# Value matmuls of a sparse attention step: four rows of two heads instead of two rows of four, with the rest of the step's jobs moved to other positions

## The chip, the cores and the metric

The kernel runs on one core of a Trainium2 chip. The metric is device time in microseconds (us). A core has the engines TensorE (PE; PEld is its weight load), VectorE (DVE), ScalarE (ACT), GpSimd (POOL) and SyncE (SP, which only issues DMAs here). Each works through its own instructions in order, and they wait for one another on semaphores.

## The reference

```python
scores = scale * np.matmul(q, k.transpose(0, 1, 3, 2))      # 4 batches, 8 heads, 768 tokens, 64 wide
mask = np.abs(blk_i - blk_j) <= 1                            # 24 blocks of 32 tokens
mask = mask | (blk_i == 0) | (blk_j == 0) | (blk_i == n_blocks - 1) | (blk_j == n_blocks - 1)
for qb in range(n_blocks):
    for kb in sampled_blocks[qb]:                            # three drawn blocks for each block of queries
        mask[qb * block:(qb + 1) * block, kb * block:(kb + 1) * block] = True
attn = softmax(np.where(mask, scores, -1e9))
x = (attn @ v) as (4 * 768, 8 * 64) tokens
xn = x / sqrt(mean(x * x) + 1e-06) * rms_g
out = (silu(xn @ w_gate) * (xn @ w_val)) @ w_out             # 512 -> 1536 -> 512
```

The drawn blocks differ by block of queries but not by batch or head.

## The kernel before

**Two stages.** Batch 0 is done densely with a mask (to about 78 us). Batches 1 to 3 are done sparsely, in 18 chunks of four query blocks (128 tokens): per batch five chunks of blocks 2 to 21, and one "wide" chunk of the blocks 0, 23, 1 and 22, of which 0 and 23 see all keys. The feed-forward network (FFN) of tokens that are ready runs between the attention work on PE, in both stages.

**FFN pieces.** `ffn_pieces` cuts the FFN of a group of chunks into pieces. `gate` (L737) is four matmuls of 128x128 weights with as many columns as the group has tokens (256, 384 or 512), then a tanh on ACT (L741); `val` (L748) is four more, and two DVE operations (L752 `u`, L756 `hps`); a quarter of `down` (L766) is three matmuls of 512 columns, its last one followed by an ACT copy (L771) and a store. A group of n chunks has 24 + 4n pieces. The chunks are grouped 2, 3, 4, 4, 3, 2. `enter` puts a group's pieces in a list, spread over the positions to the next group's entry; `position()`, called once at the end of each position, takes out as many as are due.

**The sparse loop** has a step for each chunk i and one more, 19 in all, and each step has ten positions. `do(n, f)` hangs a job f on position n; at each position the jobs run in the order in which they were hung, then `position()`. There is no scheduler: this order is the order on every engine. In step i stand, before the change:

- the values of chunk i−1 (L644): position 0 heads 0 to 3, position 1 heads 4 to 7. `values` takes one PSUM bank `op` for each call. For a narrow chunk each call is 32 matmuls with 128x32 weights (the exponentials of one query block) against 66 columns of gathered V, with the four query blocks in the four 32-column parts of the array; for a wide chunk it is 64.
- `normalise` (DVE, L669 and L670: the reciprocal and a product out of `op`) at positions 1 and 2; `squares` (ACT, L677) at 4, `rms_power` (POOL, L681 and L682) at 5, `x_scaled` (DVE, L698, and a transposing DMA on SP to the group's `xg`) at 7. The four chunks in `by_pe` (the last ones of two groups, and both of the last group) are turned by PE instead (`x_turned`, L707), at position 0 of the step after, the last chunk at position 9 of the last step.
- the scores of chunk i (L620), at positions 1 to 4 in four runs of two heads, or 1 to 8 in eight runs of one head (wide). A run is eight matmuls of 64 columns with whole 128x128 weights, and an exponential on ACT (L628).
- gathering for chunk i+1: K by DVE (`gather_k`, L475 on) and by ACT and POOL copies at register addresses (`sampled_k`, L485), Q by four DVE copies (`gather_q`, L500), V by indirect DMAs of POOL (`gather_v`, L512), whose first two blocks are for chunk i+2, at positions 6 and 7, into one of three buffers `vgs`.
- for the next batch: loads, casts of V on ACT, and turns of K and Q (six transposes on PE, L455, and an ACT copy) at positions 6 and 9.

A group enters at position 4 of the second step after its last chunk. PSUM has eight banks, which `bank` hands out in turn to `op`, `st`, `gp`, `vp`, `yp` and transposes.

```python
for h in range(4 * g, 4 * g + 4):
    ...
    if not wide:
        for w in range(2):
            for j in range(QB):
                mm(h, j, ex[:, j, w, :], vg[:, j, w, h, :], w, 2)
```

Of the kernel before, what the change touches and what calls it, by code (L numbers as in the profile page):

```python
# [9 lines left out]
FP32 = mybir.dt.float32  # L10
# [8 lines left out]
def kernel(  # L19
# [83 lines left out]
    def bank(shape, dtype, name):  # L103
        space, tag = ring[turn_of[0] % len(ring)]
        turn_of[0] += 1
        return space.tile(shape, dtype, name=name, tag=tag)
# [27 lines left out]
    def load_v(b, pr):  # L134
        t = vraw[(b, pr)] = ld.tile([P, 2, NC, D], FP32, name="vraw", tag="vraw", bufs=4)
        if b:
            nc.vector.memset(t[0:1, 0, 0, 0:1], 0.0)
        (nc.sync if b else nc.gpsimd).dma_start(
            out=t, in_=v[b, 2 * pr:2 * pr + 2].rearrange("e (p c) d -> p e c d", p=P))
# [491 lines left out]

    ops, stages, ssqs, rstds = {}, {}, {}, {}

    def values(i, g):
        b, qbs = chunks[i]
        wide = qbs[0] == 0
        op = bank([P, 512], FP32, "op")
        ops.setdefault(i, []).append(op)
        vg = vgs[i % 3].rearrange("p j (w h x) -> p j w h x", w=2, h=H)
        per = H // bursts(i)  # L640

        def mm(h, j, lhsT, rhs, n, of):
            at = (h % 4) * VW
            nc.tensor.matmul(out=op[j * BLK:(j + 1) * BLK, at:at + VW], lhsT=lhsT, rhs=rhs,  # L644
                             start=(n == 0), stop=(n == of - 1))

        for h in range(4 * g, 4 * g + 4):
            part = h // per
            ex = exs[(i, part // 4)][:, part % 4 * 512:(part % 4 + 1) * 512].rearrange(
                "p (h u w s) -> p h u w s", h=per, w=2, s=BLK)[:, h % per]  # L650
# [4 lines that stand above are left out]
                continue  # L655
            for n in range(NC):
                cc, w = divmod(n, 2)
                for j in range(2):
                    mm(h, j, ex[:, 2 * cc + j, w, :], Vs[b % 2][:, 2 * cc + w, h, :], n, NC)
                if n < 2:  # L660
                    for j in range(2, QB):
                        mm(h, j, ex[:, 4 + j, n, :], vg[:, j, n, h, :], n, 2)

    def normalise(i, g):
        if g == 0:
            stages[i] = work.tile([P, 2, DM], BF16, name="stage", tag="stage", bufs=2)[:, 0]
        rz = work.tile([P, 4], FP32, name="rz", tag="rz", bufs=2)
        res = ops[i][g][:, 0:4 * VW].rearrange("p (h x) -> p h x", x=VW)
        nc.vector.reciprocal(out=rz, in_=res[:, :, D])  # L669
        nc.vector.tensor_tensor(  # L670
            out=stages[i].rearrange("p (g h d) -> p g h d", g=2, h=4)[:, g],
            in0=res[:, :, 0:D], in1=rz.unsqueeze(2).to_broadcast([P, 4, D]), op=ALU.mult)

    def squares(i):
        ssqs[i] = work.tile([P, 1], FP32, name="ssq", tag="ssq", bufs=3)
        junk = work.tile([P, DM], BF16, name="junk", tag="junk", bufs=1)
        nc.scalar.activation(out=junk, in_=stages[i], func=AF.Square, accum_out=ssqs[i])  # L677

    def rms_power(i):
        rstds[i] = work.tile([P, 1], FP32, name="rstd", tag="rstd", bufs=3)  # L680
        nc.gpsimd.tensor_tensor(out=ssqs[i], in0=ssqs[i], in1=eps, op=ALU.add)  # L681
        nc.gpsimd.tensor_tensor(out=rstds[i], in0=ssqs[i], in1=mhalf[:, 0:1], op=ALU.pow)  # L682
# [5 lines left out]
    def x_scaled(i):  # L688
        g = group_of[i]
        at = (i - sgroups[g][0]) * P  # L690
        if at == 0:
            xgs[g] = work.tile([P, KD, TG], BF16, name="xg", tag="xg", bufs=2)
        xs = xss[i] = work.tile([P, DM], BF16, name="xs", tag="xs", bufs=3)
        if i in by_pe:
            nc.vector.tensor_scalar(out=xs, in0=stages[i], scalar1=rstds[i], scalar2=None,
                                    op0=ALU.mult)
            return
        nc.vector.scalar_tensor_tensor(  # L698
            out=xs, in0=stages[i], scalar=rstds[i], in1=gain, op0=ALU.mult, op1=ALU.mult)
        nc.sync.dma_start_transpose(out=xgs[g][:, :, at:at + P], in_=xs)  # L700
# [361 lines left out]
    NPOS = 10  # L1062
    entry = {}
    for g, m in enumerate(sgroups[:-1]):
        entry[(min(m[-1] + 2, NCH), 4)] = g

    def distance(i, n):

# [9 lines left out]
    for i in range(NCH + 1):  # L1078
        jobs = {}

        def do(n, f):
            jobs.setdefault(n, []).append(f)

        b, s = divmod(i, PB)
        b += 1
        nx = i + 1 if i + 1 < NCH else None
        if i == 0:
            do(0, late_pv)
            do(3, lambda: dense_scale(cur, 0))
            do(3, lambda: dense_scale(cur, 1))  # L1090
            do(5, lambda: dense_turn(cur, 0))
            do(6, lambda: dense_turn(cur, 1))
            do(6, lambda: enter_dense(cur, distance(0, 6)))
            do(4, lambda: nc.vector.memset(Qd[1], 0.0))
            do(3, lambda: load_kq(2, 3))
            do(7, lambda: gather_v(1, (2, 3)))
        else:
            do(0, lambda: values(i - 1, 0))
            do(1, lambda: normalise(i - 1, 0))
            do(1, lambda: values(i - 1, 1))  # L1100
            do(2, lambda: normalise(i - 1, 1))
            do(4, lambda: squares(i - 1))
            do(5, lambda: rms_power(i - 1))
            do(7, lambda: x_scaled(i - 1))
            if i == NCH:
                do(9, lambda: x_turned(i - 1))
            if i - 2 in by_pe:
                do(0, lambda: x_turned(i - 2))
        if i < NCH:
            n = bursts(i)  # L1110
            for part in range(n):
                do(1 + part, lambda part=part: scores(i, part))
        if b + 1 < B and s <= NP:
            if s < NP:
                do(9 if s == 0 else 0, lambda: cast_v(b + 1, s, act))
            if s > 0:
                do(6, lambda: turn(b + 1, s - 1, 0, act, True))
                do(9, lambda: turn(b + 1, s - 1, 1, act, True))
            if s == 0 and b == 1:
                do(8, lambda: nc.vector.memset(Vs[0][:, :, :, D:VW], 1.0))  # L1120
            if s == NP:
                do(0, lambda: table(b + 1))
        if nx is not None:
            at = 6 if nx == 1 else 0
            gk, gq = list(gather_k(nx, dve)), list(gather_q(nx, dve))
            if at == 0:
                for m, x in enumerate(gq):
                    do(3 + m * 2 // len(gq) * 2, x)
                do(4, gk[0])
                for x in gk[1:]:  # L1130
                    do(6, x)
            else:
                do(at, gk[0])
                for m, x in enumerate(gk[1:]):
                    do(at + 1 + m, x)
                for m, x in enumerate(gq):
                    do(at + 1 + m // 2, x)
            kact, kpool = sampled_k(nx, "act"), sampled_k(nx, "pool")
            for x in kpool:
                do(at, x)  # L1140
            for m, x in enumerate(kact):
                do(at + (m + 1) * (NPOS - 1 - at) // len(kact), x)
            if nx > 1:
                do(1, lambda: gather_v(nx, (2,)))
                do(2, lambda: gather_v(nx, (3,)))
            if nx + 1 < NCH:
                at = 6 if (nx + 1) % PB else 8
                do(at, lambda: gather_v(nx + 1, (0,)))
                do(at + 1, lambda: gather_v(nx + 1, (1,)))
        for m in range(min(6, len(by_need)) if i < 2 else 0):  # L1150
            do(m, next_address)

        bl, sl = divmod(i + 2, PB)
        if 0 < bl and bl + 2 < B and sl < NP:
            do(9, lambda: load_kq(bl + 2, sl))
        bv, sv = divmod(i + 3, PB)
        if 0 < bv and bv + 2 < B and sv < NP:
            do(7, lambda: load_v(bv + 2, sv))
        for n in range(NPOS):
            if (i, n) in entry:  # L1160
                g = entry[(i, n)]
                enter(ffn_pieces(xgs[g], sizes[g], chunk_store(sgroups[g])), distance(i, n))
            for x in jobs.get(n, ()):
                x()
            position()
# [35 lines left out]
```

## Time and profile before

| | |
|---|---|
| runs | 309.20, 309.18, 309.12 us; median 309.18 |
| profiled execution | 309.54 us, of which the span from first to last instruction 307.8 |
| granted TensorE clock, mean | 0.994 |
| busy: DVE, ACT, POOL | 215.2 (70%), 198.9 (65%), 147.1 (48%) |
| sparse values on PE, L644 | 1344 matmuls, mean 196 ns each, in flight together |
| sparse scores on PE, L620 | 672 matmuls of 64 columns |
| FFN on PE: L737, L748, L766 | busy 81.6, 81.3 and 72.0 us |
| exponential of a score run, L628 | 84 on ACT, 600 ns each |

A profile row names the line, the engine, the operation, the tile written and those read, how often, its busy time and the mean of one, and then the idle time of the engine ahead of such instructions with what ended most of it. "issue" is time in which the engine waited for nothing that the profile shows. Matmuls are pipelined, so their durations overlap: what one costs PE is read from the distance between starts.

### The profile page before, as it was taken

To read this page: it belongs to the slowest core of one execution; us is meant where nothing else is said; L and a number is where in the kernel's file an instruction comes from. 1 tells how busy PE (TensorE), PEld (TensorE's weight loads), DVE (VectorE), ACT (ScalarE), POOL (GpSimd) and SP (SyncE) were. 2 spreads that over 40 slices of the span, in tenths; PEclk is the share of its full clock that TensorE was granted. 3 is DMA by queue.
4 is the path that set the end of the run, shared out by engine and by line. 5 is a ranking of instruction groups with operands and counts; after the bars stand their busy time and mean duration, and the time that the engine had idled before them with its cause. 6 is when DMAs were issued, how large, how long until landed. Compare 5 with 4: busy or idle time off the path is not lost.

```text
span 307.8 us, 9872 instructions
## 1 busy us (share of the span) xinstructions
PE 284.4 (92%) x3871; PEld 187.8 (61%) x3871; DVE 215.2 (70%) x596; ACT 198.9 (65%) x467; POOL 147.1 (48%) x244
## 2 busy tenths in 40 slices
PE   7899999978969889998899898899999999999995
PEld 6677885767548657765566454454445455555683
DVE  7888798667847757963999377877449991396480
ACT  4896775666738787876898786662675575633331
POOL 9858243582746364884887542816550710000000
PEclk9999999999989999999999999999999999999999
DMA  7999999999663287598997654415543233100202
GB/s 137 290 208 201 207 227 281 257 298 227 133 200 86 76 205 267 105 250 227 141 250 205 202 163 116 119 44 148 157 156 87 78 83 100 58 2 0 104 1 68
DMA packets 37426, 47.44 MB, mean 154 GB/s; under 512 B 11184, under 2 KB 29380, under 8 KB 37380
## 3 DMA queue, kind: packets, MB, share of 16 engines
q0 software_dynamic: 21184, 32.60, 48.3%
q1 hardware_dynamic: 16132, 14.18, 15.9%
q8 instruction: 30, 0.49, 0.6%
q14 instruction: 16, 0.13, 0.2%
q10 hardware_dynamic: 64, 0.03, 0.0%
HBM read 46.45 MB, written 8.83 MB: 180 GB/s over the span
## 4 chain that ended last, share of the span: by engine, by line
PE 77%; DMA 8%; DVE 5%; issue 5%; POOL 2%; ACT 1%; ACTq 0%; DVEq 0%; POOLq 0%
PE gp L737 19%; PE vp L748 19%; PE yp L766 17%; PE st L620 7%; PE op L644 6%; DMA gain<-in_moe_rms_g_dram 4%; PE st L527 3%; PE tqk L455 2%; DMA kbf<-in_k_dram 2%; DMA xg<-xs 2%; PE op L536 2%; DVE u L752 1%; DVE hps L756 1%; DVE junk L570 1%; POOL kbf L126 1%
## 5 line engine op out<-in xcount | busy, mean ns | idle before, releaser
L737 PE MATMUL gp<-xg,wg 128*128 128x256 bf16 (+2 forms) x432 | 81.6, 309 | 2.3 <-ACT yo L771 1.1
L748 PE MATMUL vp<-xg,wv 128*128 128x256 bf16 (+2 forms) x432 | 81.3, 310 | 2.1 <-DVE u L752 1.2
L741 ACT ACTIVATE th<-gp 128x256 bf16<-128x256 f32 (+2 forms) x108 | 50.0, 463 | 44.0 <-PE gp L737 30.3
L512 POOL DMA_INDIRECT vg<-vtab,vidx x66 | 66.9, 1014 | 18.2 <-issue 13.6
L766 PE MATMUL yp<-wo,hps 128*128 128x512 bf16 (+1 forms) x300 | 72.0, 371 | 0.2 <-issue 0.2
L752 DVE SCALAR_TENSOR_TENSOR u<-th,gp 128x256 bf16<-128x256 bf16 (+2 forms) x108 | 54.5, 505 | 24.4 <-ACT th L741 20.9
L628 ACT ACTIVATE ex<-st 128x512 bf16<-128x512 f32 x84 | 50.4, 600 | 31.3 <-PE st L620 29.9
L756 DVE TENSOR_TENSOR hps<-u,vp 128x256 bf16<-128x256 bf16 (+2 forms) x108 | 55.1, 510 | 18.7 <-PE vp L748 3.3
L737 PEld LDWEIGHTS <-wg 128*128 128x128 bf16 x432 | 39.6, 98 | 20.5 <-issue 3.9
L748 PEld LDWEIGHTS <-wv 128*128 128x128 bf16 x432 | 39.6, 98 | 20.3 <-issue 3.4
L681 POOL TENSOR_TENSOR ssq<-ssq,eps 128x1 f32<-128x1 f32 x18 | 3.5, 195 | 86.6 <-ACT junk L677 86.5
L766 PEld LDWEIGHTS <-hps 128*128 128x128 bf16 x300 | 26.0, 98 | 20.9 <-issue 0.5
L530 ACT ACTIVATE ex<-st 128x768 bf16<-128x768 f32 x42 | 33.3, 813 | 5.3 <-PE st L527 4.9
L644 PEld LDWEIGHTS <-ex 128*32 128x32 bf16 x1344 | 16.2, 95 | 21.8 <-issue 20.1
L644 PE MATMUL op<-vg,ex 128*32 128x66 bf16 x1056 | 20.8, 196 | 7.1 <-issue 6.8
L771 ACT ACTIVATE yo<-yp 128x512 f32<-128x512 f32 (+1 forms) x25 | 14.6, 584 | 17.1 <-PE yp L766 16.8
L527 PE MATMUL st<-wide_q,wide_k 88*128 88x256 bf16 x144 | 23.0, 272 | 1.5 <-DVE wide_q L345 1.1
L669 DVE RECIPROCAL rz<-op 128x4 f32<-128x4 f32 x36 | 6.4, 177 | 15.4 <-PE op L644 9.7
L620 PE MATMUL st<-wide_q 128*128 128x64 bf16 x256 | 16.0, 197 | 0.6 <-issue 0.6
L620 PEld LDWEIGHTS <-wide_q 128*128 128x128 bf16 x256 | 12.9, 101 | 5.6 <-issue 0.8
L527 PEld LDWEIGHTS <-wide_k 88*128 88x128 bf16 x144 | 12.9, 97 | 5.3 <-DVE wide_q L345 2.0
L670 DVE TENSOR_TENSOR stage<-op,rz 128x256 bf16<-128x256 f32 x36 | 15.3, 425 | 1.2
(147 smaller groups left out, 385.4 us busy)
## 6 DMA issues: line engine op xcount, KB each, us to landing
out_dram<-yo SPq DMA_DIRECT2D x20, 256.0 KB
vraw<-in_v_dram SPq DMA_DIRECT2D x12, 384.0 KB
kbf<-in_k_dram POOLq DMA_DIRECT2D x15, 192.0 KB
vtab<-Vs POOLq DMA_DIRECT2D x3, 792.0 KB
qbf<-in_q_dram POOLq DMA_DIRECT2D x12, 192.0 KB
vraw<-in_v_dram POOLq DMA_DIRECT2D x4, 384.0 KB
wg<-in_moe_w_gate_dram POOLq DMA_DIRECT2D x4, 384.0 KB
wv<-in_moe_w_val_dram POOLq DMA_DIRECT2D x4, 384.0 KB
```

Source lines behind the costliest of these rows:

```text
L512: nc.gpsimd.indirect_dma_start(vgs[i % 3][:, j, :], None, vtab[b][:], bass.IndirectOffsetOnAxis(ap=vidx[:, qbs[j]:qbs[j] + 1], axis=0))
L527: nc.tensor.matmul(out=at[:, e], lhsT=KT0[0:KR, h, jt * P:(jt + 1) * P], rhs=QT0[0:KR, h, c0 * P:(c0 + 2) * P], start=True, stop=True)
L530: nc.scalar.activation(out=ex[:, 3 * part:3 * (part + 1), :], in_=at[:, 0:3], func=AF.Exp, scale=SCALE)
L620: nc.tensor.matmul(out=st[:, at:at + UN], lhsT=lhsT, rhs=Qd[i % 2][:, h, :, :, j * HB:(j + 1) * HB].rearrange("p a w s -> p (a w) s"), sta ...
L628: nc.scalar.activation(out=ex.rearrange("p (u s w) -> p u s w", s=HB, w=2), in_=st.rearrange("p (u w s) -> p u s w", s=HB, w=2), func=AF.E ...
L644: nc.tensor.matmul(out=op[j * BLK:(j + 1) * BLK, at:at + VW], lhsT=lhsT, rhs=rhs, start=(n == 0), stop=(n == of - 1))
L737: nc.tensor.matmul(out=gp[:, 0:tg], lhsT=wg[:, c, f * P:(f + 1) * P], rhs=xg[:, c, 0:tg], start=(c == 0), stop=(c == KD - 1))
L741: nc.scalar.activation(out=th[:, 0:tg], in_=gp[:, 0:tg], func=AF.Tanh, scale=0.5)
L748: nc.tensor.matmul(out=vp[:, 0:tg], lhsT=wv[:, c, f * P:(f + 1) * P], rhs=xg[:, c, 0:tg], start=(c == 0), stop=(c == KD - 1))
L752: nc.vector.scalar_tensor_tensor(out=u[:, 0:tg], in0=th[:, 0:tg], scalar=1.0, in1=gp[:, 0:tg], op0=ALU.add, op1=ALU.mult)
L756: nc.vector.tensor_tensor(out=hps[f][:, 0:tg], in0=u[:, 0:tg], in1=vp[:, 0:tg], op=ALU.mult)
L766: nc.tensor.matmul(out=yp, lhsT=hps[f][:, tt * P:(tt + 1) * P], rhs=wo[:, f, lo:hi], start=(f == 0), stop=(f == NF - 1))
```

## The change

`values` is called with a quarter (two heads) instead of a half, and stands at positions 0, 1, 2 and 3; two quarters share a bank. `normalise` goes to positions 2 and 4, the score runs to 4 to 7 (wide: 2 to 9), squares, power and scaling to 6, 7 and 9 (in the last step 5, 5 and 6, with `x_turned` at 8), the group entries from position 4 to 6. The turns of K and Q go to 2 and 8, and the Q gather, the K copies, the first V gathers and the load of V to other positions. For the chunk after the first the positions of its gathers stay.

```diff
-    def values(i, g):
+    def values(i, quarter):
...
-        op = bank([P, 512], FP32, "op")
-        ops.setdefault(i, []).append(op)
+        if quarter % 2 == 0:
+            ops.setdefault(i, []).append(bank([P, 512], FP32, "op"))
+        op = ops[i][-1]
...
-        for h in range(4 * g, 4 * g + 4):
+        for h in range(2 * quarter, 2 * quarter + 2):
...
-        entry[(min(m[-1] + 2, NCH), 4)] = g
+        entry[(min(m[-1] + 2, NCH), 6)] = g
...
-            do(0, lambda: values(i - 1, 0))
-            do(1, lambda: normalise(i - 1, 0))
-            do(1, lambda: values(i - 1, 1))
-            do(2, lambda: normalise(i - 1, 1))
-            do(4, lambda: squares(i - 1))
-            do(5, lambda: rms_power(i - 1))
-            do(7, lambda: x_scaled(i - 1))
+            for quarter in range(4):
+                do(quarter, lambda quarter=quarter: values(i - 1, quarter))
+            do(2, lambda: normalise(i - 1, 0))
+            do(4, lambda: normalise(i - 1, 1))
+            sooner = 1 if i == NCH else 0
+            do(6 - sooner, lambda: squares(i - 1))
+            do(7 - 2 * sooner, lambda: rms_power(i - 1))
+            do(9 - 3 * sooner, lambda: x_scaled(i - 1))
             if i == NCH:
-                do(9, lambda: x_turned(i - 1))
+                do(8, lambda: x_turned(i - 1))
             if i - 2 in by_pe:
-                do(0, lambda: x_turned(i - 2))
+                do(2, lambda: x_turned(i - 2))
...
-                do(1 + part, lambda part=part: scores(i, part))
+                do((4 if n == 4 else 2) + part, lambda part=part: scores(i, part))
...
-                do(6, lambda: turn(b + 1, s - 1, 0, act, True))
-                do(9, lambda: turn(b + 1, s - 1, 1, act, True))
+                do(2, lambda: turn(b + 1, s - 1, 0, act, True))
+                do(8, lambda: turn(b + 1, s - 1, 1, act, True))
...
             if at == 0:
                 for m, x in enumerate(gq):
-                    do(3 + m * 2 // len(gq) * 2, x)
-                do(4, gk[0])
-                for x in gk[1:]:
-                    do(6, x)
+                    do(m * 2 // len(gq) * 3, x)
+                do(1, gk[0])
+                for m, x in enumerate(gk[1:]):
+                    do(6 + m, x)
+                for m, x in enumerate(kact):
+                    do((0, 1, 1, 2, 3, 3, 8, 9)[m], x)
...
-                at = 6 if (nx + 1) % PB else 8
+                at = 5 if (nx + 1) % PB else 8
...
-            do(7, lambda: load_v(bv + 2, sv))
+            do(9, lambda: load_v(bv + 2, sv))
```

More of the change, by code (lines that the diff above doesn't have):

```diff
@@ L1125 @@
             gk, gq = list(gather_k(nx, dve)), list(gather_q(nx, dve))
+            kact, kpool = sampled_k(nx, "act"), sampled_k(nx, "pool")
+            for x in kpool:
+                do(at, x)
             if at == 0:
                 for m, x in enumerate(gq):
-                    do(3 + m * 2 // len(gq) * 2, x)
-                do(4, gk[0])
-                for x in gk[1:]:
-                    do(6, x)
+                    do(m * 2 // len(gq) * 3, x)
[4 more added lines that the diff above has]
+                    do((0, 1, 1, 2, 3, 3, 8, 9)[m], x)
             else:
@@ L1137 @@
                     do(at + 1 + m // 2, x)
[L1138 to L1142, printed above, removed]
+                for m, x in enumerate(kact):
+                    do(at + (m + 1) * (NPOS - 1 - at) // len(kact), x)
             if nx > 1:
```

## The prediction

> **What bounds the kernel now.** I read the page's engine totals and chain first, then the waits of TensorE, then its timeline round one pair of value bursts, then the windows table.
>
> ```profile
> PE 284.4 (92%) x3871; PEld 187.8 (61%) x3871; DVE 215.2 (70%) x596; ACT 198.9 (65%) x467; POOL 147.1 (48%) x244
> PE 77%; DMA 8%; DVE 5%; issue 5%; POOL 2%; ACT 1%; ACTq 0%; DVEq 0%; POOLq 0%
> ```
>
> TensorE (PE) is the bound: 92% busy and 77% of the chain. "issue 5%" on the chain is time in which the engine waited for nothing that the profile names. The waits of PE from 78 us to the end say where that is:
>
> ```profile
> PE op L644 <- issue: 8.0, 16, 1.0
> PE st L620 <- issue: 1.5, 4, 0.5
> PE gp L737 <- ACT yo L771: 1.1, 1, 1.1
> PE gp L737 <- DMA xg<-xs: 0.8, 1, 0.8
> ```
>
> Columns: total us, times, longest. The waits on other engines are two, 1.9 us together; nearly all the rest is the value matmuls (L644), without a releaser. The view counts idle time after the end of the last matmul, so the loss is larger than its 8.0. The timeline shows one pair of bursts:
>
> ```profile
> 183.88 1.03 PE L748 MATMUL vp<-xg,wv 128*128 128x512 bf16 x4
> 184.84 0.43 PE L644 MATMUL op<-vg,ex 128*32 128x66 bf16 x32
> 185.20 1.04 PE L737 MATMUL gp<-xg,wg 128*128 128x512 bf16 x4
> 186.16 0.28 PE L644 MATMUL op<-vg,ex 128*32 128x66 bf16 x12
> 186.86 0.23 PE L644 MATMUL op<-vg,ex 128*32 128x66 bf16 x2 [0.42 <-issue]
> 187.58 0.39 PE L644 MATMUL op<-vg,ex 128*32 128x66 bf16 x18 [0.50 <-issue]
> ```
>
> The first burst of 32 goes through in one piece; the second stops twice, and restarts come about 0.73 us apart with a handful of instructions each. I call such a burst starved. Taking from the same timeline every step between two starts inside a burst that is over 0.1 us, I get 12.5 us in 11 of the 33 value bursts (3.3 us in the one at 85.2). Steps above the usual pace in the score matmuls (L620) just behind give 3.0 us more, those in the FFN matmuls just behind 1.4 us: **17 us**. The pattern: of the twelve first bursts of 32 none is starved, of the twelve second ones six are, of three that lie two in one piece (64) all are, of six of the wide step two are. A step's first gap comes no earlier than about 60 instructions (a weight load and a matmul each) after its first burst began. A score stretch, 16 + 8 instructions per 1.10 us (22 per us), runs for eight positions without a gap. So instructions seem to reach PE more slowly than dense small ones are used up, with a reserve.
>
> The windows view (columns: length, then busy us and count of PE, PEld, DVE, ACT, POOL, then the granted clock, DMA share, GB/s):
>
> ```profile
> 80.00:98.00 18.00, 14.84 (x213) 10.69 (x210) 10.89 (x32) 11.35 (x33) 10.97 (x19) 0.91 0.58 156
> 146.00:156.00 10.00, 8.99 (x147) 6.07 (x145) 9.26 (x24) 8.68 (x24) 8.59 (x14) 1.00 1.00 196
> 233.00:249.00 16.00, 16.00 (x200) 7.95 (x199) 14.93 (x33) 8.97 (x20) 6.14 (x10) 1.00 0.34 91
> ```
>
> Clock 0.91 in the first: after the largest gap cluster the FFN matmuls run at half pace for 3.4 us, 1.1 us lost. In the second DVE is 93% busy: there is little to win there. In the third PE is full and DVE 93%.
>
> **The change part by part.** No matmul is added or taken away: 3871 matmuls before and after in the built order, 1344 of them L644.
>
> *More, shorter value bursts (a cost).* A run of L644 matmuls, uninterrupted in PE's order, stands 33 times in the order before and 68 times after: 52 of 16, four of 32 (a position without FFN piece between), twelve of 32 in the three wide steps. One burst of 32 costs 0.46 us: four 512-column matmuls take 0.86 us (189.25 to the next score matmul at 190.11), so the one at 183.88 is through at 184.74, the burst starts at 184.84, the next FFN matmul at 185.20. Inside, 32 starts span 0.43 minus the last one's own 0.20, 0.23 us, 7.5 ns each, 0.24 for 32. So 0.46 − 0.24 = 0.22 us is fixed: 0.10 going in, the rest coming out. The score matmuls, which use the whole array, go in and out of FFN matmuls with 0.00 to 0.01 (188.15 + 0.86 = 189.01, start 189.02). The wide burst at 201.30 takes 0.93 with 64 at 11 ns: 0.22 again. PE works in order and nothing hides it: 35 × 0.215 = **+7.5 us**.
>
> *Half the density (a gain of unknown size).* Before, the values of a narrow step with one FFN piece between and the first score run are 64 + 8 + 64 + 16 = 152 instructions in some 1.9 us (80 per us). After, each of four positions has 32 + 8 in 0.33 + 0.86 us with 512 columns (34 per us), up to 53 per us with 256 columns; the wide step has 64 + 6 in 1.2 us for four positions (57 per us). Both ends: nothing goes (0), or all goes (17 + 1.1 for the clock = −18.1). Within them, for a narrow step: a reserve of about 64 (the first gap) and arrival at x per us. At the starved rate, ten per 0.73 us or 14 per us, the overdraft before is 152 − 1.9·14 − 64 = 61, after 160 − 4.8·14 − 64 = 29: half goes. At 25 per us, about what scores show as sustained, it is 40 before and none after: all goes. Wide steps keep more than half, but they hold only 2.4 us of the 12.5. I take 70%, between the two: 0.7 × 17 = −11.9, and the clock's 1.1, since a cluster of 4 us should not form: **−13.0 us**.
>
> *What then binds.* In 146 to 165 DVE has 9.26 + 8.36 of 19 us and PE's gaps there were about 2; with these gone and three steps' extra switches in, PE would need 18.2 and DVE 17.6, too near to overlap fully. I give back **+1.0**. Elsewhere DVE has slack or PE was full already.
>
> *Places.* Scores go from positions 1–4 to 4–7, their exponentials (0.60 us on ACT) with them, and their values come in the next step's 0–3: six positions of lead as before. The bank of a result now stays open over two quarters; counting bank allocations in the order, the ninth one, which needs it back, comes two positions behind the normalise that frees it, as before. Squares, power and scaling go two later (but for the last step) and the group entries too, so the transposing DMA keeps seven positions; its one late landing (0.8 in the waits) may stay: 0. Gathers one earlier: POOL's gather of the chunk after next now stands two positions behind the quarter whose buffer it overwrites, not five; behind it in POOL's queue are the next gather and the power. POOL is 48% busy, the values that use the vectors are over a step away: 0, and if it does wait, the power is late and DVE's scaling behind it, up to 2 us a step in which nothing of that chunk is due. The K and Q turns, K copies, Q gathers and the V load (SP) go to other positions with as many instructions: 0, hidden beside FFN matmuls. In the last step x is turned 13 FFN pieces (8.4 us) behind the last value burst, where it was 18 (11.7 us); the chain there took 7 us: 0, or +1 if DVE is late.
>
> Sum: +7.5 − 13.0 + 1.0 = −4.5. The profiled execution took 309.54 (span 307.8 and 1.7 around it), 0.36 above the runs' median 309.18. 309.54 − 4.5 = 305.0, in the runs' terms **304.7 us**.
>
> **The rivals.**
> 1. *The gaps don't follow density* (slower). They come by time or by place in the program, and half bursts meet as many. For: after 223 us bursts as dense as those before run without one; in the step at 97.6, 175 instructions pass before the first gap. Against: none of the twelve first bursts has one. Then only the switches are left: 309.2 + 7.5 = 316.7. It decides once under 7.5 of the 18.1 us goes, about 41%. The Trainium skill (Runtime: NRT & Kernel Launch, section Instruction fetch mechanics) bears on it: it says that straight-line instruction fetch is sequential, in blocks of 256 instructions, and hidden, because issue is slower than the refill. By that rule the gaps are no backlog of instructions and spreading them wins nothing, 316.7; the trace speaks against it with gaps in straight-line bursts that no semaphore explains, but shows no cause.
> 2. *Starved rate throughout.* Half of 17 goes: −8.5, −1.1, +7.5, +1: 308.1.
> 3. *Nearly all goes* and DVE keeps up: 309.2 − 18.1 + 7.5 = 298.6, with a little left 300.
> 4. *A new wait.* Normalise of the first half, now behind two quarters, frees its bank late where DVE is 93% busy, and a gate waits. At one pair of L752 and L756 (1.0 us by their rows) in half of the 18 steps that is 9 us, and with some of it beside other waits 7 on top of 304.7: 312. No wait of PE on L669/L670 stands in the view now, which speaks against it.
>
> **How the numbers follow.** Forecast (302 to 307.3) 0.40; rival 3 (298.6 to 302) 0.13; rival 2 (307.3 to 310) 0.15, of which faster 0.07, same 0.05, slower 0.03; rival 1 (312 to 317) 0.20; rival 4 (309.8 to 314) 0.12. A measurement can tell 0.2%, 0.6 us, from no change. Faster 0.40 + 0.13 + 0.07 = 0.60, same 0.05, slower 0.03 + 0.20 + 0.12 = 0.35. The range 299.5 to 314 leaves out about 0.05 below and 0.13 above. The forecast's own range is 302 to 307.3.
>
> **What would show it.** In the profile after: 68 value bursts with 0.10 us ahead of each and as much behind; the "issue" wait of L644 down from 8.0 to 2 or 3 us; granted clock 1.00 in 80 to 98 us; no wait of PE on DVE. Wrong: as much "issue" as before, spread over shorter bursts (rival 1), or a wait on L669/L670 or on L771 of several us (rival 4).

## The result and the profile after

The changed kernel takes **331.75 us** (median of 329.98 to 333.11), the kernel before in the same comparison 309.19: ratio 1.071 (95% interval 1.065 to 1.078). The forecast was 304.7. The profiled execution of the changed kernel took 332.4 with a span of 330.6, 22.8 more than the span before (307.8). Where a kernel's runs include one that is over 1.5% longer than its fastest, the medians below include it and the ratios leave it out. Lines behind the edit of `values` shift by one in the new file: L645 is the old L644, L670/L671 the old L669/L670, L738/L749/L753/L757 the old L737/L748/L752/L756.

The page of the changed kernel, engine totals, granted clock by fortieths of the span, chain:

```profile
PE 298.6 (90%) x3871; PEld 188.9 (57%) x3871; DVE 217.7 (66%) x596; ACT 201.0 (61%) x467; POOL 145.8 (44%) x244
PEclk9999999979998999997999999969999999999999
PE 74%; DVE 12%; issue 6%; DMA 4%; ACT 2%; another core or an unknown queue 0%; POOL 0%; ACTq 0%; DVEq 0%
```

The share of DVE on the chain went from 5% to 12%, "issue" did not fall, and the clock row dips under 9 in four places, where it did in one; the first of the four lies at 66 to 74 us, in the dense stage. The waits of PE from 78 us on:

```profile
PE op L645 <- issue: 7.7, 16, 0.7
PE vp L749 <- DVE stage L671: 4.6, 5, 2.1
PE st L620 <- DVE rz L670: 1.8, 1, 1.8
PE vp L749 <- issue: 1.4, 3, 0.6
PE gp L738 <- DVE rz L670: 1.3, 2, 0.7
PE st L620 <- DVE stage L671: 0.9, 1, 0.9
```

Two readings. The first line is nearly as large as before (8.0): the gaps without a releaser, which half bursts were to shrink, are still there. And the lines that name L670 and L671, the normalise, were not in the view before. The timeline of PE in the first sparse step shows the gaps at work on bursts of 16:

```profile
85.08 0.30 PE L645 MATMUL op<-vg,ex 128*32 128x66 bf16 x16
85.32 0.61 PE L749 MATMUL vp<-xg,wv 128*128 128x256 bf16 x4
85.86 0.30 PE L645 MATMUL op<-vg,ex 128*32 128x66 bf16 x16
86.10 0.61 PE L738 MATMUL gp<-xg,wg 128*128 128x256 bf16 x4
86.64 0.21 PE L645 MATMUL op<-vg,ex 128*32 128x66 bf16 x3
87.29 0.24 PE L645 MATMUL op<-vg,ex 128*32 128x66 bf16 x4 [0.44 <-issue]
88.05 0.31 PE L645 MATMUL op<-vg,ex 128*32 128x66 bf16 x9 [0.52 <-issue]
```

The first two go through, the third stops twice. The next lines, a step later, are those of DVE and PE that bear on the wait, out of a view of all engines (start, duration, idle time with its releaser in brackets):

```profile
101.44 0.55 DVE L471 COPY wide_q<-KT 128x1536 bf16<-128x1536 bf16 x1
...
101.91 0.17 DVE L670 RECIPROCAL rz<-op 128x4 f32<-128x4 f32 x1
102.12 0.42 DVE L671 TENSOR_TENSOR stage<-op,rz 128x256 bf16<-128x256 f32 x1
...
102.60 0.61 PE L738 MATMUL gp<-xg,wg 128*128 128x256 bf16 x4 [0.57 <-DVE rz L670]
...
103.41 0.59 DVE L500 COPY wide_q<-QN 64x512 bf16<-64x512 bf16 x2
104.03 0.42 DVE L753 SCALAR_TENSOR_TENSOR u<-th,gp 128x256 bf16<-128x256 bf16 x1
...
104.89 0.17 DVE L670 RECIPROCAL rz<-op 128x4 f32<-128x4 f32 x1
105.10 0.42 DVE L671 TENSOR_TENSOR stage<-op,rz 128x256 bf16<-128x256 f32 x1
...
105.59 1.03 PE L749 MATMUL vp<-xg,wv 128*128 128x256 bf16 x4 [2.14 <-DVE stage L671]
```

DVE works in order: ahead of normalise stand the K copy (L471) and the Q copies (L500) that the change moved to positions 0 to 3, and the u and hps of the FFN pieces. The bank that the gate at 102.60 needs is free only when the first normalise is through, and the `val` at 105.59 waits 2.1 us for the second. Its four matmuls then take 1.03 where they took 0.61: the clock is halved. The windows of the changed kernel show that (columns as above):

```profile
98.00:108.00 10.00, 6.71 (x96) 5.03 (x95) 7.45 (x20) 6.74 (x20) 4.49 (x6) 0.85 0.44 123
...
209.00:225.00 16.00, 13.58 (x194) 6.66 (x192) 8.78 (x20) 5.96 (x17) 5.56 (x9) 0.79 0.30 77
```

To add it up I took from the timelines every step between two matmul starts, from the first value burst to the end, less the usual pace (0.42 ns for a column between full matmuls, as in the 0.86 us for four of 512; 0.10 us at each end of a value burst, up to 0.02 inside), and sorted what is left by what the profile says ended it:

| us | before | after | difference |
|---|---|---|---|
| ahead of the first value burst (the dense stage and step 0) | 83.2 | 85.1 | +1.9 |
| usual pace, with the ends of 33 and 68 bursts | 197.8 | 204.4 | +6.6 |
| gaps without a releaser in value bursts | 12.3 | 11.7 | −0.6 |
| such gaps in scores and FFN behind them | 4.0 | 4.1 | +0.1 |
| waits on normalise | 0 | 10.9 | +10.9 |
| matmuls at half clock | 1.6 | 4.8 | +3.2 |
| ACT, DMA, small | 5.2 | 6.0 | +0.8 |

The differences come to 22.9, of 22.8 in the span. The first 1.9 need not be the change's, though it moves the scores of step 0: a second profile of the kernel before (experiment 2) reaches its first value burst at 84.6 us too, with a half-clock stretch of 3.4 us at 68 us; the changed kernel has one at 67.5.

### The profile page after: what moved, and what is told of

Same layout as the page of the kernel before. It is cut to its first block, busy times and chain, and to the rows that moved or that the text cites. A ratio compares the mean times of both kernels' runs of the same rounds, so it can differ in the third digit from the quotient of the medians.

```text
span 330.6 us, 9845 instructions
## 1 busy us (share of the span) xinstructions
PE 298.6 (90%) x3871; PEld 188.9 (57%) x3871; DVE 217.7 (66%) x596; ACT 201.0 (61%) x467; POOL 145.8 (44%) x244
## 4 chain that ended last, share of the span: by engine, by line
PE 74%; DVE 12%; issue 6%; DMA 4%; ACT 2%; another core or an unknown queue 0%; POOL 0%; ACTq 0%; DVEq 0%
PE yp L767 18%; PE vp L749 18%; PE gp L738 17%; PE op L645 7%; PE st L620 5%; DMA gain<-in_moe_rms_g_dram 4%; PE st L527 3%; PE tqk L455 2%; DVE u L753 2%; DVE hps L757 2%; PE op L536 2%; PE unread L228 1%; DVE junk L570 1%; DVE stage L671 1%; DVE wide_q L345 1%
## 5 line engine op out<-in xcount | busy, mean ns | idle before, releaser
L749 PE MATMUL vp<-xg,wv 128*128 128x256 bf16 (+2 forms) x432 | 83.0, 314 | 8.3 <-DVE stage L671 4.6
L753 DVE SCALAR_TENSOR_TENSOR u<-th,gp 128x256 bf16<-128x256 bf16 (+2 forms) x108 | 54.5, 505 | 47.4 <-ACT th L742 46.0
L738 PE MATMUL gp<-xg,wg 128*128 128x256 bf16 (+2 forms) x432 | 82.9, 313 | 1.7 <-DVE rz L670 1.3
L512 POOL DMA_INDIRECT vg<-vtab,vidx x66 | 65.7, 996 | 28.0 <-issue 14.3
L767 PE MATMUL yp<-wo,hps 128*128 128x512 bf16 (+1 forms) x300 | 75.0, 376 | 0.7 <-issue 0.5
L757 DVE TENSOR_TENSOR hps<-u,vp 128x256 bf16<-128x256 bf16 (+2 forms) x108 | 55.0, 510 | 20.4 <-PE vp L749 7.9
L628 ACT ACTIVATE ex<-st 128x512 bf16<-128x512 f32 x84 | 49.6, 598 | 30.7 <-PE st L620 25.9
L749 PEld LDWEIGHTS <-wv 128*128 128x128 bf16 x432 | 38.9, 99 | 24.9 <-DVE stage L671 5.5
L738 PEld LDWEIGHTS <-wg 128*128 128x128 bf16 x432 | 39.0, 99 | 19.6 <-issue 1.9
L645 PEld LDWEIGHTS <-ex 128*32 128x32 bf16 x1344 | 18.0, 96 | 34.9 <-issue 33.3
L645 PE MATMUL op<-vg,ex 128*32 128x66 bf16 x1056 | 24.9, 197 | 3.8 <-issue 3.5
L527 PE MATMUL st<-wide_q,wide_k 88*128 88x256 bf16 x144 | 24.1, 281 | 1.8 <-DVE wide_q L345 1.4
L620 PEld LDWEIGHTS <-kg 128*128 128x128 bf16 x272 | 13.8, 103 | 9.5 <-DVE rz L670 2.1
L620 PE MATMUL st<-Qd,kg 128*128 128x64 bf16 x272 | 15.7, 200 | 2.7 <-DVE rz L670 1.8
L671 DVE TENSOR_TENSOR stage<-op,rz 128x256 bf16<-128x256 f32 x36 | 15.3, 424 | 1.2
L620 PEld LDWEIGHTS <-wide_q 128*128 128x128 bf16 x256 | 12.4, 98 | 6.1 <-issue 1.2
```

The costliest lines, as they stand in the source:

```text
L512: nc.gpsimd.indirect_dma_start(vgs[i % 3][:, j, :], None, vtab[b][:], bass.IndirectOffsetOnAxis(ap=vidx[:, qbs[j]:qbs[j] + 1], axis=0))
L527: nc.tensor.matmul(out=at[:, e], lhsT=KT0[0:KR, h, jt * P:(jt + 1) * P], rhs=QT0[0:KR, h, c0 * P:(c0 + 2) * P], start=True, stop=True)
L620: nc.tensor.matmul(out=st[:, at:at + UN], lhsT=lhsT, rhs=Qd[i % 2][:, h, :, :, j * HB:(j + 1) * HB].rearrange("p a w s -> p (a w) s"), sta ...
L628: nc.scalar.activation(out=ex.rearrange("p (u s w) -> p u s w", s=HB, w=2), in_=st.rearrange("p (u w s) -> p u s w", s=HB, w=2), func=AF.E ...
L738: nc.tensor.matmul(out=gp[:, 0:tg], lhsT=wg[:, c, f * P:(f + 1) * P], rhs=xg[:, c, 0:tg], start=(c == 0), stop=(c == KD - 1))
L749: nc.tensor.matmul(out=vp[:, 0:tg], lhsT=wv[:, c, f * P:(f + 1) * P], rhs=xg[:, c, 0:tg], start=(c == 0), stop=(c == KD - 1))
```

## The experiments

The runs fell on several chips, and these are of two kinds: on two of them, called quiet here, the kernel before takes 290 to 291.5 us, on the others 307 to 314, as in the result above. So each ratio is to the kernel before on the same chip. Of the four chips whose number is on record (3 and 12 quiet, 0 and 2 not) only chip 2 was used twice, both times with gaps, so whether it is the chip or the hour that decides is not shown. "Gaps" are those without a releaser inside value bursts, counted as in the table.

### 1. One part of the change back at a time (quiet chip)

The first three edits are to the changed kernel, the fourth to the kernel before. The expectations were written for a chip on which the kernel before takes 309 us, and the changed kernel itself was run on no quiet chip; so these runs are compared with the kernel before there and with one another.

**Values in halves, in the places of the change**

```diff
+    def values_bank(i):
+        ops.setdefault(i, []).append(bank([P, 512], FP32, "op"))
...
-        if quarter % 2 == 0:
-            ops.setdefault(i, []).append(bank([P, 512], FP32, "op"))
...
+                if quarter % 2 == 0:
+                    do(quarter, lambda: values_bank(i - 1))
-                do(quarter, lambda quarter=quarter: values(i - 1, quarter))
+                do(quarter // 2 * 2 + 1, lambda quarter=quarter: values(i - 1, quarter))
```

> The changed kernel with two quarters of the values in one piece (positions 1 and 3, their banks still taken at 0 and 2, everything else where the change put it): 36 value bursts instead of 68. Theory S (each burst pays 0.21 us for going in and out): 32 x 0.21 = 6.8 us less, 331.8 to 325. Rival D (the denser bursts are starved more, as the prediction had it): 6.8 less, but some 10 us more of gaps without a releaser, 335. Waits of PE on the normalise (L670, L671) as many as in the changed kernel by either.

Measured: 303.98 against 291.05, ratio 1.044 (1.039 to 1.049). No gap at all in 36 bursts, of which six of 64, so nothing speaks of density here; waits on normalise 12.2 us, by far the most of the 13 lost.

**Normalise one position sooner**

```diff
-            do(2, lambda: normalise(i - 1, 0))
-            do(4, lambda: normalise(i - 1, 1))
+            do(1, lambda: normalise(i - 1, 0))
+            do(3, lambda: normalise(i - 1, 1))
```

> The changed kernel with normalise at positions 1 and 3, right behind the quarter that completes its half, instead of 2 and 4. Theory W (PE waits some 10 us because the bank of a half comes free late, and half of the extra time at half clock follows from these waits): the waits on L670 and L671 go, 10 us and 3 us of half clock less, 318 to 322. Rival C (normalise is late because the copies of Q and K stand ahead of it on DVE and ACT, so that one position does not help): 328 to 332.

**The copies of Q and K back**

```diff
-                    do(m * 2 // len(gq) * 3, x)
-                do(1, gk[0])
+                    do(3 + m * 2 // len(gq) * 2, x)
+                do(4, gk[0])
...
-                    do((0, 1, 1, 2, 3, 3, 8, 9)[m], x)
+                    do((m + 1) * (NPOS - 1) // len(kact), x)
```

> The changed kernel with the Q and K copies of the next chunk (DVE and ACT) back at the positions they had before the change (3 to 9 instead of 0 to 3 and 6 to 9). Rival C: the waits of PE on L670 and L671 go, 318 to 322. Theory W in its narrow form (only normalise's own position counts): 329 to 332.

Measured: 300.28, ratio 1.033 (1.030 to 1.036), and 300.20, ratio 1.033 (1.031 to 1.036). Waits of PE on normalise with normalise sooner:

```profile
PE vp L749 <- DVE stage L671: 0.8, 1, 0.8
PE gp L738 <- DVE stage L671: 0.7, 1, 0.7
```

and with the copies back:

```profile
PE vp L749 <- DVE stage L671: 2.2, 2, 1.7
PE st L620 <- DVE stage L671: 1.1, 2, 0.8
PE gp L738 <- DVE stage L671: 1.1, 1, 1.1
```

By the count between starts 2.4 and 5.2 us, against 12.2 in the run with halves on the same chip. Both causes take part: normalise's position and what stands ahead of it on DVE (one position sooner, it also stands ahead of the K copy and the second pair of Q copies). Neither half clock nor a gap is left in these two runs.

**Only the quarters, all else as before**

`values` is cut into quarters as in the change; its calls:

```diff
-            do(0, lambda: values(i - 1, 0))
-            do(1, lambda: normalise(i - 1, 0))
-            do(1, lambda: values(i - 1, 1))
-            do(2, lambda: normalise(i - 1, 1))
+            for quarter in range(4):
+                do(quarter, lambda quarter=quarter: values(i - 1, quarter))
+            do(1, lambda: normalise(i - 1, 0))
+            do(3, lambda: normalise(i - 1, 1))
```

> The kernel before with the values alone in four quarters at positions 0 to 3, normalise at 1 and 3, all else where it was: 69 value bursts instead of 33. Theory S with gaps that do not depend on density: 36 x 0.21 = 7.6 us more, 316.8. Rival D (density sets the gaps, as predicted): 7.6 more, 12 of the 17 us of gaps less, 305. Theory W: no more than 1 us of waits on normalise, since it stands right behind its quarter and ahead of the copies.

Measured on the quiet chip: 296.65, ratio 1.020 (1.018 to 1.022), no gaps, no wait on normalise. The 5.6 us are the price of the switches, less some other waits that went; experiment 3 takes them apart.

### 2. The whole change and its moves (a chip with gaps)

> The changed kernel, unedited, beside the kernel before on the chip of this call. In the last call the kernel before took 291 us, not 309, and no experiment had a gap without a releaser in its value bursts. Theory P (these gaps belong to the conditions of a chip or a session, not to the density of bursts): where the kernel before takes 291, the changed one has none either and takes 291 + 7.4 (35 bursts at 0.21) + 6 to 9 (waits on normalise) = 304 to 307; where it takes 309, about 331 again with both kinds. Rival D (density makes the gaps): with no gaps before there is nothing to save, but the waits would be the same, so it gives the same total; the two differ where the kernel before has gaps.

> The kernel before, unedited, for its profile on the chip of this call. Theory P: all or none of the 12.5 us of gaps inside L644 bursts, and a span of about 308 or 290.

> The changed kernel with normalise at 1 and 3 and also the Q and K copies back where they were: what is left of the change are the quarters and the moves of scores, turns, V gathers and group entries. If normalise and copies are the whole of the waits (theory W and rival C together), waits of PE on L670 and L671 are under 1 us and the ratio to the kernel before is 1.025 (only the 7.4 us of switches); if the moves of the scores and turns have a price of their own, it stays at 1.033 as with either edit alone.

> As the last, and with the values in halves again (36 bursts): only the moves of scores, turns, V gathers and entries are left. If these are harmless, the ratio to the kernel before is 1.00 to 1.005; if they have a price, it is above 1.01, and this run gives it alone.

The edits are those above, together. The kernel before: 310.55, 10.2 us of gaps. The changed kernel: 327.54, ratio 1.050 (1.040 to 1.059), gaps 7.9, waits on normalise 10.3. Normalise sooner and copies back: 322.41, ratio 1.039 (1.029 to 1.049), gaps 10.5, normalise 0.6. With halves too: 316.42, ratio 1.023 (1.013 to 1.032), gaps 9.3, normalise 0.7. Waits of PE in the run with normalise sooner and copies back:

```profile
PE op L645 <- issue: 7.6, 14, 1.2
PE st L620 <- issue: 2.7, 6, 1.1
PE tqk L455 <- DVE u L753: 0.7, 1, 0.7
```

The waits on normalise fell from 10.3 to 0.6 us, as expected, but the time fell by only 3 us by the ratios (5 by the medians), not 10: more gaps (7.9 to 10.5) and some 3 us more of other waits on DVE took up the rest. 33, 36 and 68 bursts have 10.2, 9.3 and 10.5 us of gaps. The last step, 68 to 36 bursts, is worth 6.0 us by the medians and 5.1 by the ratios, about what 32 switches at 0.2 cost. What is left, the moves of scores, turns, gathers and entries, costs 5.9 us by the medians and 7.0 by the ratio (interval 4.2 to 9.8); expected were 0 to 1.5 if they are harmless. Some 3 us of it are more waits on DVE's u and hps, 1.1 more on the transposing DMA. What in these moves makes them I did not take apart.

### 3. Quarters alone, and what the gaps hang on

Two rows of runs, the first on a quiet chip:

> The kernel before, unedited, once more for its profile beside the next three. Theory P: its gaps without a releaser in the value bursts are about 10 to 12 us where it takes 309, and none where it takes 291.

> The kernel before with the values alone in quarters, as in the fourth experiment, on the chip of this call. Where the kernel before takes 309: theory P plus S, 7.6 us more and as many gaps (8 to 12 us in the value bursts), 317; rival D, 12 us of gaps less, 305. Where it takes 291: 296 to 298 again, and the profile of the kernel before beside it then shows why it was 5.6 and not 7.6.

> The kernel before without the V gathers of the chunks from the fourth on (60 of 66 indirect DMAs left out in all but the first three chunks; the values use older vectors, so part of the computation is left out). Theory M (the gaps come when the V gathers, by POOL's work or by their DMA traffic, hold up what PE needs): on a chip where the kernel before has gaps, they are gone from the fourth chunk on, some 8 to 12 us less. Rival N (gaps have nothing to do with the gathers): within 3 us of the kernel before, gaps as many.

> The kernel before with x turned by PE for all 18 chunks instead of four, so that no transposing DMA is left. The turns cost PE 14 x 4 transposes of 0.06 us and DVE 14 products of some 0.5 us: 3 to 4 us more if DVE or PE shows all of it. Theory T (the gaps come behind the transposing DMAs; in the profile before six of eleven gap clusters begin within 3 us of one): on a chip with gaps most of 10 us go, in sum 5 to 8 us less. Rival N: gaps as many, 2 to 4 us more.

The two new edits, each to the kernel before:

```diff
-            if qbs[j] not in (0, NB - 1):
+            if qbs[j] not in (0, NB - 1) and i < 3:
                 nc.gpsimd.indirect_dma_start(
```

```diff
-    by_pe = [*sgroups[-1], sgroups[1][-1], sgroups[2][-1]]
+    by_pe = list(range(NCH))
```

Measured: the kernel before 291.09; quarters 296.53, ratio 1.020 (1.018 to 1.022); without later gathers 290.94, ratio 1.000 (0.9985 to 1.0008); without transposing DMAs 294.18, ratio 1.011 (1.009 to 1.013). No gaps in value bursts in any. The waits of PE in the kernel before on this chip have no "issue" line left; the longest are

```profile
PE vp L748 <- DVE u L752: 0.5, 1, 0.5
PE st L620 <- DVE stage L670: 0.5, 1, 0.5
```

Between starts, the usual pace went from 197.2 to 204.3, 7.1 us for 36 more bursts, 0.20 each; the span rose by 5.6, since 0.4 us less lay ahead of the first value burst and 1.1 us of other waits went.

The second row, with the last two on another chip, all with gaps:

> The changed kernel, unedited. Where the kernel before takes 291 (no gaps): 7.4 for the switches and 5 to 9 for the waits on normalise, 303 to 307, ratio 1.04 to 1.055, and no gap in the value bursts. Where it takes 309: 327 to 332 with gaps of 8 to 12 us.

> The kernel before with the values alone in quarters. Where the kernel before takes 309 (gaps), rival D gives 305, since the half bursts are starved less, and theory P plus S gives 315 to 318 with 8 to 12 us of gaps in the value bursts. Where it takes 291: 296.5 once more.

> The kernel before without the V gathers from the fourth chunk on (the values use older vectors). Where the kernel before has gaps: theory M, they are gone after 110 us, 297 to 301; rival N, 307 to 311 with gaps as many. Where it has none: 291, as in the last call.

> The kernel before with x turned by PE for all chunks. Where the kernel before has gaps: theory T, most of the 10 us in the value bursts go, 302 to 305; rival N, they stay, 311 to 314. Where it has none: 294, as in the last call.

> The changed kernel, unedited. Where the kernel before takes 291 (no gaps): 7.4 for the switches, less some 2 that the kernel before's own waits cover, and 5 to 9 for the waits on normalise, 302 to 306. Where it takes 307 to 313: 326 to 332.

> The kernel before with the V rows of the chunks from the fourth on loaded by plain DMAs of SP, as many bytes (128 rows of 2112) to the same places from the same table, but 128 rows in a row instead of the drawn ones (so the values use other rows), instead of 60 indirect DMAs of POOL. Where the kernel before has gaps: theory Mt (the traffic makes them) leaves 8 to 12 us of gaps and 307 to 313 us; theory Mp (POOL's indirect DMAs, how they are made or queued, make them) has none after 110 us and takes 297 to 303. Where it has none: 290 to 294.

```diff
+            if qbs[j] not in (0, NB - 1) and i >= 3:
+                nc.sync.dma_start(out=vgs[i % 3][:, j, :], in_=vtab[b][8 * qbs[j]:8 * qbs[j] + P, :])
-            if qbs[j] not in (0, NB - 1):
+            elif qbs[j] not in (0, NB - 1):
                 nc.gpsimd.indirect_dma_start(
```

| run | kernel before | this | ratio (95%) | gaps, us |
|---|---|---|---|---|
| the changed kernel, third time | 312.1 | 331.25 | 1.061 (1.055 to 1.066) | 13.0 |
| quarters alone | 312.1 | 314.98 | 1.008 (1.005 to 1.011) | 5.0 |
| no later gathers | 312.1 | 300.40 | 0.963 (0.960 to 0.967) | 4.0 |
| no transposing DMA | 312.1 | 316.00 | 1.015 (1.010 to 1.020) | 11.5 |
| the changed kernel, fourth time | 309.49 | 326.99 | 1.057 (1.048 to 1.066) | 11.9 |
| plain V loads | 309.49 | 297.94 | 0.964 (0.957 to 0.970) | 1.2 |

The gaps hang on the indirect DMAs. The two edits leave out 54 of the 66, not 60 as the expectations say: the traces of these runs hold 12, the last at 90 us. The waits of PE from 110 us on, first in the kernel before:

```profile
PE op L644 <- issue: 5.5, 12, 0.5
```

With plain V loads, all there is:

```profile
PE vp L750 <- DVE u L754: 0.6, 1, 0.6
PE gp L739 <- DVE u L754: 0.2, 1, 0.2
```

and without later gathers likewise no value burst waits. As many bytes over SP's queue bring no gaps, so it is not the number of bytes as such. The transposing DMAs are not it either: theory T fell. Whether it is POOL's making of the descriptors or the drawn rows that are read, these runs do not tell, nor why two chips show none of it.

The traces kept say the same burst by burst. In the kernel before, PE's stops stand beside indirect DMAs on POOL (lines of other instructions left out):

```profile
86.69 0.97 POOL L512 DMA_INDIRECT vg<-vtab,vidx  x1 [0.16 <-issue]
...
87.29 0.27 PE L644 MATMUL op<-vg,ex 128*32 128x66 bf16 x5 [0.49 <-issue]
...
87.96 0.95 POOL L512 DMA_INDIRECT vg<-vtab,vidx  x1 [0.30 <-issue]
88.01 0.28 PE L644 MATMUL op<-vg,ex 128*32 128x66 bf16 x5 [0.46 <-issue]
```

Take for each value burst the time from 0.5 us ahead of it to its usual end. In 24 of the 33 bursts of the kernel before an indirect DMA runs on POOL in that time; all 11 bursts with gaps are among them, and the other nine bursts have none. In the ten profiles with gaps whose gathers are all in, 91 bursts have gaps, every one with such a DMA, and none of the 252 bursts without one has a gap. An indirect DMA alone is not enough: 204 bursts have one and no gap, and on a quiet chip 24 of the 33 bursts have one too and none has a gap.

Quarters alone cost 2.4 us by the ratio (interval 1.6 to 3.3) on a chip with gaps and 5.4 to 5.6 on a quiet one. So smaller bursts do save some 3 us there, of 18 that lie between the two kinds of chips. In the value bursts gaps fell to 5.0, against 10.2 and 12.3 in the two profiles of the kernel before with gaps (one is of another chip, the other's chip is not on record). Part of that came back elsewhere: PE's waits without a releaser in L620 are 2.2 us in that run, 1.4 to 1.5 in the kernel before, and the scores waited 3.0 us for copies of K on POOL and ACT, 0.4 at most before.

## Why the prediction was wrong

- **More, shorter bursts: right.** Forecast +7.5, 35 at 0.215. Clean bursts of 16 last 0.33 us between their neighbours, as worked out, those of 32 in the wide steps 0.57; the sums give 6.6 in the result and 7.1 for 36 in the quiet pair.
- **Half the density: the step that failed.** I took 70% of 17 us as saved, 11.9, between ends of 0 and 18.1. The result has −0.5, and quarters alone save some 3. I read "the first burst is never starved, the second often" as a reserve that dense instructions use up. Against it stood what I wrote under the first rival: no gaps after 223 us with bursts as dense. That was the better clue: of the eight bursts after 223 us one has an indirect DMA beside it, of the 25 ahead of it 23. Gaps need the indirect DMAs; without these, the same bursts in the same order have none. What density adds stays open: in the order of the change 68 bursts had 7.9 to 13.0 us of gaps, in the order of the kernel before 69 had 5.0 in the one run with gaps.
- **The clock: wrong in sign.** Forecast −1.1; +3.2. I let the half-clock stretch go with the gaps. In the changed kernel two stretches (at 149.5 and 217.7 us) follow gaps that stayed, one (at 105.1) follows waits on normalise: 13.7 us at half clock in the sparse stage, where there was one stretch of 3.4. A fourth, of 3.4, lies in the dense stage and is part of the 1.9 ahead of the first value burst.
- **What then binds: mis-sized by ten.** Forecast +1.0 for a DVE that is too near its limit, and a rival (the fourth) at 7 with chance 0.12; measured 10.9 on normalise. I counted positions between normalise and the allocation that needs its bank (two, as before) and costed that at nothing. Two positions are not a fixed time on DVE: what counts is what DVE and ACT have queued ahead of normalise, and the change put the copies of Q and K there. The view before said no PE wait on L669/L670 and I took that as a margin; it held only for the order that DVE's jobs had then.
- **Places: wrong.** I put every moved job at 0. Together they cost 6 to 7 us on a chip with gaps even with normalise and copies put back.
- **The rivals.** Rival 1 (gaps do not follow density, 316.7) and rival 4 (a new wait, 312) both came true; I had them as alternatives, and they add up: 309.2 + 6.6 + 10.9 + 3.2 and 1.9 ahead of the first value burst. The range, to 314, had room for rival 4 alone but not for both. With the rule of the Trainium skill that stood beside rival 1 (Runtime: NRT & Kernel Launch, Instruction fetch mechanics) the quiet chips agree: straight-line bursts without a gap. On the others there are gaps, and they come with the indirect DMAs; whether by way of the instruction fetch no run here shows. The profile's busiest instruction queue (q8) moved as much on either kind of chip, 30 packets and 0.49 MB in the kernel before.

No version tried beats the kernel before. The run with plain V loads took 0.964 of the time on a chip with gaps but reads other rows, so it only shows what the indirect DMAs cost there.

## What to carry to other kernels

Before a change is built on a theory of a gap that the profile puts down to nothing, list for each burst, those with gaps and those without, what the other engines do: here that takes no run, and it points at the indirect DMAs. Then try another chip, and each kind of DMA left out: in two runs that shows that burst length is at most a small lever. When jobs move, read each engine's own queue ahead of the one instruction that frees a shared buffer; a distance in positions says nothing if copies slip in between. And causes that each make a change slower are not rivals to choose from: ask whether they can all hold.

## What the runs showed of the hardware

The same program takes 290 to 291.5 us on two chips and 307 to 314 on others, with no gap without a releaser in the value bursts on the first and 10 to 12 us of them on the others. Within a gap PE restarts some 0.73 us apart, with two to five matmuls each time in the lines shown. Replacing 54 of 66 indirect DMAs by plain ones of as many bytes takes some 11 us off on a chip with gaps, and leaving them out changes nothing (ratio 1.000) on a quiet one. A run of 128x32 matmuls among full ones costs 0.20 to 0.22 us beyond its own streaming (bursts of 16 last 0.33 us, of 32 0.46). The clock halved for 3.4 or 6.8 us at a time in the changed kernel's sparse stage, behind steps between two matmul starts of which none was longer than 2.3 us; in the profile before the longest was 1.25.
